# A gated recurrence followed by soft mixture-of-experts slots: a full, overlapping last group of tokens, a fourth decay buffer, another place for the copies of h, and another timetable for the weight loads

## The chip, the cores and the metric

The kernel runs on one core of one Trainium2 chip. A core has five engines that run side by side, each with its own in-order queue of instructions: TensorE (PE) multiplies and transposes, VectorE (DVE), ScalarE (ACT) and GpSimd (POOL) work elementwise, and SyncE (SP) issues transfers. Transfers run on 16 DMA engines. SBUF is the working memory of 128 partitions, PSUM the memory that TensorE writes to. The metric is the device time of one execution in microseconds; less is better. The times of the kernel before are 239.87, 241.03 and 241.69 us.

## The reference

Two stages. The first is a recurrence over 5056 tokens, for each of 4 batches and 256 channels; the second is a soft mixture of experts over all 20224 tokens, with 8 experts of 4 slots each.

```python
sig = 1.0 / (1.0 + np.exp(-f_logit))
f = lower_bound + (1.0 - lower_bound) * sig
i = 1.0 - f
for t in range(S):                       # y has the shape of x: (4, 5056, 256)
    h = f[:, t] * h + i[:, t] * x[:, t]
    y[:, t] = h

x = y.reshape(B * S, D)
logits = x @ phi                         # 20224 x 32
d = softmax of logits over the tokens (axis 0)
slot_input = (d.T @ x).reshape(E, S_per_e, D)
slot_out[e] = np.maximum(slot_input[e] @ w1[e], 0.0) @ w2[e]      # F = 1024
c = softmax of logits over the slots (axis 1)
out = c @ slot_out                       # 20224 x 256
```

All tokens must have gone through the recurrence and into the slots before the first output row can be made.

## The kernel before, in words

**Tiling.** The tokens of a batch are cut into groups of G = 1024, which is two halves (H = 2) of 512 (W), and a half is 128 partitions with R = 4 tokens each. 5056 tokens make four full groups and one of 960 tokens, which is held as two halves of 480 tokens on 120 partitions (`rows(4)` = 120). A unit is one group of one batch; there are 20 units, numbered `n = 4 * group + batch`.

**Phase one** (lines 115 to 332) is a software pipeline written out by hand: the loop at line 285 runs over steps n, and each step issues work of several units. For unit m:

- `load` (step m-5): one transfer of `f_t` and one of `x_t`, from SyncE's queue; three buffers each, so that `f_t` of unit m waits until the gate of unit m-3 is done, and `x_t` until its product is.
- `gate` (step m-2): ScalarE, sigmoid to `s_t`. `enter` (step m-2): GpSimd, product `u_t = s_t * x_t`.
- `s_to_channels` (end of step m-2) and `u_to_channels` (step m-1): eight TensorE transposes each, into PSUM tiles `sp` (one buffer, shared with the logits `lg`) and `up` (two buffers).
- `decay` (step m-1): two ScalarE instructions that write the decays `a` (three buffers), one for each half of the channels.
- `scan` (step m): two VectorE scans, one for each half of the channels, each starting from the last value of unit m-4 (same batch, group ahead). The last group, whose halves don't lie end to end, takes four scans.
- `to_tokens` and `keep_tokens` (step m+1): for each half of the tokens four TensorE transposes of `h` into `hp` (one buffer), and a copy to `ht`, by ScalarE for half 0 and by VectorE for half 1.

When a group's four units are scanned (`g1`), TensorE makes the logits and ScalarE the exponentials (`exps`, which needs another activation table, so the table is loaded before and after it). A step later (`g2`) the weights are transposed and copied (`et`), GpSimd sums them by row (`row_sums`), and the slots are accumulated (`slots`), with their second half a step later still (`g3`).

Every engine takes its work in the order in which the loop issues it. In the part of a step that the change touches, this order is: `load(n+5)`, `gate(n+2)`, `enter(n+2)`, weight loads, `u_to_channels(n+1)`, `decay(n+1)`, `weights_to_tokens(g2, 0)`, `scan(n, 0)`, `to_tokens(n-1, 0)`, `keep_tokens(n-1, 0)`, `keep_weights(g2, 0)`, and so on. So on ScalarE the copy of `h` of unit n-1 stands behind the decays of unit n+1.

**Weights.** The 16 weight loads (8 of `w1`, 8 of `w2`, each cast from float32 to bfloat16 on the way, 512 KB as written) are issued from GpSimd's queue at the steps of the table `W_AT`, behind that step's `enter`. Twelve of the sixteen are issued at step 17, behind the product of unit 19; the last four of `w2` go into load buffers that have come free.

**Tail and phase two.** The experts work on the slots (lines 335 to 408): the first layer needs all `w1`, and the second takes `w2` expert by expert (line 399). Then the output loop (line 415) multiplies the stored exponentials by the experts' result, scales by the row sums on VectorE or ScalarE, and stores each half unit from SyncE's queue: 128 partitions of 4 KB, in the last group 120.

Of the kernel before, what the change touches and what calls it, by code (L numbers as in the profile page):

```python
# [18 lines left out]
def kernel(  # L19
# [10 lines left out]
    nc = tc.nc  # L30
# [5 lines left out]
    P = 128  # L36
# [7 lines left out]
    n_unit = n_grp * B  # L44


    def rows(g):
        return min(P, (S - g * G) // (R * H))

    ctx.enter_context(tc.manual_schedule())  # L50

# [57 lines left out]
        nc.gpsimd.dma_start(out=w2_sb[e], in_=w2_r[e])  # L109


    W_AT = {8: 1, 13: 1, 15: 1, 16: 1, 17: 2 * E - 4}
    w_next = [0]

    with tc.tile_pool(name="sup", bufs=2) as sup, \
         tc.tile_pool(name="apool", bufs=3) as apool, \
         tc.tile_pool(name="hpool", bufs=6) as hpool, \
         tc.tile_pool(name="htok", bufs=7) as htok, \
         tc.tile_pool(name="etok", bufs=2) as etok, \
# [13 lines left out]

        def load(n):
            g, b = divmod(n, B)
            n_p = rows(g)
            fs[n] = ld.tile([P, H, R, D], F32, name="f_t", tag="f_t")
            xs[n] = ld.tile([P, H, R, D], F32, name="x_t", tag="x_t")
            for k in halves(n):
                for t, src in ((fs, f_logit), (xs, x)):  # L140
                    src = src[b, ds(g * G, n_p * R * H)]
                    src = src.rearrange("(h p r) d -> p h (r d)", h=H, r=R)
                    dst = t[n].rearrange("p h r d -> p h (r d)")
                    nc.sync.dma_start(out=dst[:n_p, k], in_=src[:, k])


        def gate(n):
            n_p = rows(n // B)
            sts[n] = sup.tile([P, H, R, D], BF16, name="s_t", tag="s_t")
            for k in halves(n):  # L150
                nc.scalar.activation(sts[n][:n_p, k], fs[n][:n_p, k], ACT.Sigmoid, scale=-1.0)  # L151

        def enter(n):
            n_p = rows(n // B)
            uts[n] = sup.tile([P, H, R, D], BF16, name="u_t", tag="u_t")
            eng = nc.vector if n == 0 else nc.gpsimd
            for k in halves(n):
                eng.tensor_tensor(uts[n][:n_p, k], sts[n][:n_p, k], xs[n][:n_p, k], ALU.mult)  # L158

        def to_channels(n, t, ps):  # L160
            n_p = rows(n // B)
            t = t.bitcast(F32)
            for h in range(H):
                for r in range(R):
                    nc.tensor.transpose(ps[:, h, :n_p, r], t[:n_p, h, r], ident_f[:n_p, :n_p])  # L165
            ps = ps.rearrange("c h p r -> c (h p r)").bitcast(BF16)
            return ps.rearrange("c (h t o) -> c h t o", h=H, o=DC)

        def s_to_channels(n):
            ps = ps_s.tile([P, H, P, R], F32, name="sp", tag="sp")  # L170
            sps[n] = to_channels(n, sts.pop(n), ps)

        def u_to_channels(n):
            ps = psu.tile([P, H, P, R], F32, name="up", tag="up")
            ups[n] = to_channels(n, uts.pop(n), ps)

        def flat(t, n_t):

            if n_t == W:
                return [t.rearrange("c h t -> c (h t)")]  # L180
            return [t[:, h, :n_t] for h in range(H)]

        def decay(n):
            n_t = rows(n // B) * R
            sp = sps.pop(n)
            for o in range(DC):
                a = apool.tile([P, H, W], F32, name="a", tag="a")
                nc.scalar.activation(a[:, :, :n_t], sp[:, :, :n_t, o], ACT.Identity,  # L188
                                     scale=nomlb[:, ds(o, 1)], bias=1.0)
                decays[n, o] = a  # L190

        def scan(n, o):
            n_t = rows(n // B) * R
            if o == 0:
                hs[n] = hpool.tile([P, H, W, DC], BF16, name="h", tag="h")
            carry = hs[n - B][:, H - 1, ds(W - 1, 1), o] if n >= B else 0.0
            for h, a, u in zip(flat(hs[n][:, :, :, o], n_t), flat(decays.pop((n, o)), n_t),
                               flat(ups[n][:, :, :, o], n_t)):
                nc.vector.tensor_tensor_scan(h, a, u, carry, ALU.mult, ALU.add)  # L199
                carry = h[:, ds(n_t - 1, 1)]  # L200

        def to_tokens(n, h):
            n_p = rows(n // B)
            hp = ptp.tile([P, R, P], F32, name="hp", tag="tp")
            hps[n, h] = hp
            hw = hs[n].bitcast(F32).rearrange("c h (p r) o -> c h p (r o)", r=R)
            for r in range(R):
                nc.tensor.transpose(hp[:n_p, r], hw[:, h, :n_p, r], ident_f)  # L208

        def keep_tokens(n, h):  # L210
            n_p = rows(n // B)
# [3 lines left out]
            copy(hts[n][:n_p, h].rearrange("p r d -> p (r d)").bitcast(F32),  # L215
                 hps.pop((n, h))[:n_p].rearrange("p r c -> p (r c)"))


        def logits(g):
            n_t = rows(g) * R  # L220
            lg = ps_s.tile([P, H, W], F32, name="lg", tag="sp")
            for h in range(H):
                for o in range(DC):
                    for b in range(B):
                        nc.tensor.matmul(lg[ds(b * NS, NS), h, :n_t], phi[:, o],  # L225
                                         hs[g * B + b][:, h, :n_t, o],
                                         start=o == 0, stop=o == DC - 1,
                                         skip_group_check=True)
            return lg

        def exps(g, lg):
            n_t = rows(g) * R
            nc.scalar.activation(etall[:, g, :, :n_t], lg[:, :, :n_t], ACT.Exp,
                                 accum_out=csum[:, ds(g, 1)])

        def weights(g, h):
            n_p = rows(g)
            return etall[:, g, h, :n_p * R].rearrange("s (p r) -> s p r", r=R)

        def weights_to_tokens(g, h):  # L240
            ew = weights(g, h)
            for r in range(R):
                nc.tensor.transpose(ep_ps[:rows(g), r], ew[:, :, r], ident)

        def keep_weights(g, h):
            n_p = rows(g)
            if h == 0:
                ets[g] = etok.tile([P, H, R, B, NS], BF16, name="et", tag="et")
            nc.vector.tensor_copy(ets[g][:n_p, h].rearrange("p r b s -> p (r b s)"),  # L249
                                  ep_ps[:n_p].rearrange("p r s -> p (r s)"))  # L250

        def row_sums(g):
            n_p, w = rows(g), NS // 2
            part = ets[g][:n_p].rearrange("p h r b s -> p (h r b) s")
            while w:
                if w == 1:
                    dst = rsum[:n_p, g].rearrange("p h r b -> p (h r b)").unsqueeze(2)
                else:
                    dst = rsp.tile([P, H * R * B, w], F32, name="rs", tag=f"rs{w}")[:n_p]
                nc.gpsimd.tensor_tensor(dst, part[:, :, :w], part[:, :, ds(w, w)], ALU.add)  # L260
                part, w = dst, w // 2

        def slots(g, h):
            n_p = rows(g)
# [20 lines left out]
        for n in range(-AHEAD, n_unit + 4):  # L285
            def has(m):
                return 0 <= m < n_unit
# [124 lines left out]
    with tc.tile_pool(name="pout", bufs=4, space=PSUM) as pout, \  # L412
         tc.tile_pool(name="osb", bufs=6) as osb:
        n_op = 0
        for n in range(n_unit):
            g, b = divmod(n, B)
            n_p = rows(g)
            dst = out[ds(b * S + g * G, n_p * R * H)]
            dst = dst.rearrange("(h p r) d -> p h r d", h=H, r=R)
            for h in range(H):  # L420
                op = pout.tile([P, R, D], F32, name="op", tag="op")
                ew = etall[:, g, h, :n_p * R].rearrange("s (p r) -> s p r", r=R)
                for r in range(R):
# [51 lines left out]
```

## Time and profile before

| | |
|---|---|
| median of three runs | 241.03 us |
| profiled execution | 241.04 us |
| its span, first to last instruction | 238.9 us |
| mean granted TensorE clock | 0.748 |
| busy: TensorE, VectorE, ScalarE, GpSimd | 144.7, 150.3, 135.5, 103.5 us |
| moved by DMA | 70.73 MB, mean 296 GB/s |
| scans of unit 0 begin, of unit 19 end | 11.65 us, 153.54 us |
| experts' result ready (`slot_out`) | 179.5 us |

Times in a profile are microseconds from the first instruction of the span. A line of the timeline has start and duration, engine, line of the kernel, operation, output and inputs, the number of merged instructions, and in brackets how long the engine was idle before it and what ended that idle time. "PEclk" or "granted clock" is the TensorE clock that the throttle granted, as a part of full speed. The DMA share is the mean busy share of the 16 DMA engines. A wait for several things is put down to the one that came last by the profile; where the engine named had long been done, it was another, often a transfer.

### The profile page before, as it was taken

To read this page: it belongs to the slowest core of one execution; us is meant where nothing else is said; L and a number is where in the kernel's file an instruction comes from. 1 tells how busy PE (TensorE), PEld (TensorE's weight loads), DVE (VectorE), ACT (ScalarE), POOL (GpSimd) and SP (SyncE) were. 2 spreads that over 40 slices of the span, in tenths; PEclk is the share of its full clock that TensorE was granted. 3 is DMA by queue.
4 is the path that set the end of the run, shared out by engine and by line. 5 is a ranking of instruction groups with operands and counts; after the bars stand their busy time and mean duration, and the time that the engine had idled before them with its cause. 6 is when DMAs were issued, how large, how long until landed. Compare 5 with 4: busy or idle time off the path is not lost.

```text
span 238.9 us, 2824 instructions
## 1 busy us (share of the span) xinstructions
PE 144.7 (61%) x1040; PEld 107.2 (45%) x1040; DVE 150.3 (63%) x128; ACT 135.5 (57%) x172; POOL 103.5 (43%) x68
## 2 busy tenths in 40 slices
PE   0637607663866568554868648378739877758600
PEld 0526607552754457543757537244515433325400
DVE  0465698886698966986888867722306654645520
ACT  3467807798578948799477934040106655254350
POOL 1057764627988289747995367166000000000000
PEclk9999975897699958998597968755875555555555
DMA  6999999995969986999999927999934999999995
GB/s 219 417 410 409 410 410 411 406 407 197 348 229 412 320 298 256 298 219 223 231 252 232 248 50 145 210 215 212 212 66 174 395 404 406 402 405 407 346 340 193
DMA packets 19357, 70.73 MB, mean 296 GB/s; under 512 B 1872, under 2 KB 1872, under 8 KB 19344
## 3 DMA queue, kind: packets, MB, share of 16 engines
q1 hardware_dynamic: 16752, 62.13, 72.0%
q0 software_dynamic: 2304, 8.39, 17.7%
q8 instruction: 8, 0.13, 0.2%
q10 hardware_dynamic: 288, 0.03, 0.1%
q14 instruction: 5, 0.04, 0.1%
HBM read 58.23 MB, written 20.71 MB: 330 GB/s over the span
## 4 chain that ended last, share of the span: by engine, by line
DMA 33%; ACT 22%; DVE 17%; PE 12%; issue 7%; SPq 3%; POOL 2%; ACTq 0%; DVEq 0%; POOLq 0%
DMA out_dram<-ob 12%; ACT a L188 9%; DMA x_t<-in_moe_w_dram 8%; DMA f_t<-in_f_logit_dram 8%; DVE h L199 8%; PE hp L208 5%; DMA w_sb_91<-in_moe_w_dram 5%; ACT ht L215 4%; PE sp L165 4%; ACT ob L432 3%; DVE ht L215 3%; DVE ob L435 3%; ACT s_t L151 3%; SPq L443 3%; DVE phi L79 2%
## 5 line engine op out<-in xcount | busy, mean ns | idle before, releaser
L158 POOL TENSOR_TENSOR u_t<-s_t,x_t 128x2048 bf16<-128x2048 bf16 (+1 forms) x19 | 78.1, 4108 | 50.8 <-ACT s_t L151 39.6
L199 DVE TENSOR_TENSOR_SCAN h<-a,h,up 128x1024 bf16<-128x1024 f32 (+1 forms) x40 | 74.3, 1884 | 0.3
L188 ACT ACTIVATE a<-sp,nomlb 128x1024 f32<-128x1024 bf16 (+1 forms) x40 | 42.8, 1099 | 32.9 <-PE sp L165 19.5
L208 PE MATMUL hp<-ident_f,h 128*128 128x128 f32 (+1 forms) x160 | 31.5, 327 | 33.0 <-ACT ht L215 29.2
L432 ACT ACTIVATE ob<-op,rrow 128x256 f32<-128x256 f32 (+1 forms) x68 | 26.4, 481 | 34.9 <-DVE ob L435 21.8
L151 ACT ACTIVATE s_t<-f_t 128x2048 bf16<-128x2048 f32 (+2 forms) x21 | 38.5, 1836 | 7.8 <-DMA f_t<-in_f_logit_dram 7.8
L424 PE MATMUL op<-slot_out,etall 32*128 32x256 bf16 (+1 forms) x160 | 36.4, 403 | 10.4 <-ACT ob L432 8.0
L435 DVE TENSOR_TENSOR ob<-op,rrow 128x1024 f32<-128x1024 f32 (+2 forms) x24 | 28.0, 1179 | 22.0 <-DMA out_dram<-ob 17.0
L208 PEld LDWEIGHTS hp<-ident_f,h 128*128 128x128 f32 (+1 forms) x160 | 24.2, 209 | 39.0 <-ACT ht L215 32.2
L165 PE MATMUL sp<-ident_f,s_t 128*128 128x128 f32 (+1 forms) x160 | 29.3, 342 | 15.1 <-ACT s_t L151 10.5
L424 PEld LDWEIGHTS <-etall 32*128 32x128 bf16 (+1 forms) x160 | 20.4, 146 | 26.8 <-issue 21.4
L165 PEld LDWEIGHTS sp<-ident_f,s_t 128*128 128x128 f32 (+1 forms) x160 | 23.7, 178 | 19.3 <-issue 8.3
L215 DVE COPY ht<-hp 128x512 f32<-128x512 f32 (+1 forms) x20 | 13.8, 690 | 26.5 <-PE hp L208 26.5
L165 PE MATMUL up<-ident_f,u_t 128*128 128x128 f32 (+1 forms) x160 | 27.0, 326 | 3.8 <-POOL u_t L158 3.8
L165 PEld LDWEIGHTS up<-ident_f,u_t 128*128 128x128 f32 (+1 forms) x160 | 23.8, 174 | 4.8 <-POOL u_t L158 4.8
L199 DVE TENSOR_TENSOR_SCAN h<-a,up 128x1024 bf16<-128x1024 f32 x8 | 17.8, 2273 | 5.9 <-PE up L165 5.9
L215 ACT COPY ht<-hp 128x512 f32<-128x512 f32 (+1 forms) x20 | 11.6, 582 | 8.0 <-PE hp L208 8.0
L267 PE MATMUL bank<-ht,et 128*32 128x256 bf16 (+1 forms) x160 | 8.6, 358 | 5.0 <-DVE et L249 5.0
L225 PE MATMUL lg<-h,phi 128*32 128x512 bf16 (+1 forms) x80 | 6.1, 431 | 7.0 <-ACT a L188 7.0
L267 PEld LDWEIGHTS <-et 128*32 128x32 bf16 (+1 forms) x160 | 5.0, 117 | 7.2 <-issue 6.1
L260 POOL TENSOR_TENSOR rs<-rs 128x256 f32<-128x256 f32 (+5 forms) x15 | 7.4, 491 | 1.2
L151 ACT ACT_TABLE_LOAD x5 | 6.4, 1283 | 1.7 <-PEq L459 1.7
(77 smaller groups left out, 92.4 us busy)
## 6 DMA issues: line engine op xcount, KB each, us to landing
f_t<-in_f_logit_dram SPq DMA_DIRECT2D x15, 1024.0 KB, 8.8
x_t<-in_x_dram SPq DMA_DIRECT2D x15, 1024.0 KB, 9.4
out_dram<-ob SPq DMA_DIRECT2D x30, 512.0 KB, 5.7
f_t<-in_f_logit_dram SPq DMA_DIRECT2D x4, 960.0 KB, 13.8
x_t<-in_x_dram SPq DMA_DIRECT2D x4, 960.0 KB, 14.6
out_dram<-ob SPq DMA_DIRECT2D x8, 480.0 KB, 6.6
f_t<-in_f_logit_dram SPq DMA_DIRECT2D x2, 512.0 KB, 5.0
x_t<-in_x_dram SPq DMA_DIRECT2D x2, 512.0 KB, 5.9
```

Of the source, the lines that this page charges most:

```text
L151: nc.scalar.activation(sts[n][:n_p, k], fs[n][:n_p, k], ACT.Sigmoid, scale=-1.0)
L158: eng.tensor_tensor(uts[n][:n_p, k], sts[n][:n_p, k], xs[n][:n_p, k], ALU.mult)
L165: nc.tensor.transpose(ps[:, h, :n_p, r], t[:n_p, h, r], ident_f[:n_p, :n_p])
L188: nc.scalar.activation(a[:, :, :n_t], sp[:, :, :n_t, o], ACT.Identity, scale=nomlb[:, ds(o, 1)], bias=1.0)
L199: nc.vector.tensor_tensor_scan(h, a, u, carry, ALU.mult, ALU.add)
L208: nc.tensor.transpose(hp[:n_p, r], hw[:, h, :n_p, r], ident_f)
L215: copy(hts[n][:n_p, h].rearrange("p r d -> p (r d)").bitcast(F32), hps.pop((n, h))[:n_p].rearrange("p r c -> p (r c)"))
L260: nc.gpsimd.tensor_tensor(dst, part[:, :, :w], part[:, :, ds(w, w)], ALU.add)
L267: nc.tensor.matmul(slot_ps[ds(b * NS, NS), :], ets[g][:n_p, h, r, b], hts[g * B + b][:n_p, h, r], start=(h == 0 and r == 0), stop=(h == H ...
L424: nc.tensor.matmul(op[:n_p, r], ew[ds(b * NS, NS), :, r], slot_out[ds(b * NS, NS), :], start=True, stop=True, skip_group_check=True)
L432: nc.scalar.activation(ob[:n_p, r], op[:n_p, r], ACT.Copy, scale=rrow[:n_p, g, h, r, ds(b, 1)])
L435: nc.vector.tensor_tensor(ob[:n_p, r], op[:n_p, r], rrow[:n_p, g, h, r, ds(b, 1)].broadcast_to([n_p, r.stop - r.start, D]), ALU.mult)
```

## The change

Four things are changed.

1. The last group has 1024 tokens like the others. It starts at S - G = 4032 (`first`), 64 tokens ahead of where the fourth group ends. All units load, gate and scan 1024 tokens. The fourth group, units 12 to 15, scans its 1024 tokens but uses the first 960 (`used`) in the second stage: half 0 has 128 rows, half 1 has 112. The carry of the last group is taken at token 960 of the fourth. The row sums of the fourth group are made in two parts, since its halves differ in rows.
2. The pool of the decays has four buffers instead of three.
3. `to_tokens(n-1, 0)` and `keep_tokens(n-1, 0)` stand ahead of the weight loads, `u_to_channels(n+1)`, `decay(n+1)` and `scan(n, 0)` of their step. On TensorE the four transposes come ahead of those of `u`, and on ScalarE the copy comes behind the gate and ahead of the decays.
4. Weight loads are issued at steps 2, 5, 8, 11, 13, 15 and 16, one each, and nine at step 17, instead of one each at 8, 13, 15 and 16 and twelve at 17.

```diff
+    def first(g):
+        return g * G if g < n_grp - 1 else S - G
+    def used(g):
+        return first(g + 1) - first(g) if g < n_grp - 1 else G
-    def rows(g):
-        return min(P, (S - g * G) // (R * H))
+    def rows(g, h):
+        return min(P, (used(g) - h * W) // R)
...
-    W_AT = {8: 1, 13: 1, 15: 1, 16: 1, 17: 2 * E - 4}
+    W_AT = {2: 1, 5: 1, 8: 1, 11: 1, 13: 1, 15: 1, 16: 1, 17: 2 * E - 7}
...
-         tc.tile_pool(name="apool", bufs=3) as apool, \
+         tc.tile_pool(name="apool", bufs=4) as apool, \
...
-                    src = src[b, ds(g * G, n_p * R * H)]
+                    src = src[b, ds(first(g), G)]
...
-                    nc.sync.dma_start(out=dst[:n_p, k], in_=src[:, k])
+                    nc.sync.dma_start(out=dst[:, k], in_=src[:, k])
...
-            carry = hs[n - B][:, H - 1, ds(W - 1, 1), o] if n >= B else 0.0
-            for h, a, u in zip(flat(hs[n][:, :, :, o], n_t), flat(decays.pop((n, o)), n_t),
-                               flat(ups[n][:, :, :, o], n_t)):
-                nc.vector.tensor_tensor_scan(h, a, u, carry, ALU.mult, ALU.add)
-                carry = h[:, ds(n_t - 1, 1)]
+            carry = 0.0
+            if n >= B:
+                h, t = divmod(used(n // B - 1) - 1, W)
+                carry = hs[n - B][:, h, ds(t, 1), o]
+            nc.vector.tensor_tensor_scan(
+                hs[n].rearrange("c h t o -> c (h t) o")[:, :, o],
+                decays.pop((n, o)).rearrange("c h t -> c (h t)"), ups[n][:, :, o],
+                carry, ALU.mult, ALU.add)
...
+            same = rows(g, 0) == rows(g, H - 1)
+            for k in [ds(0, H)] if same else [ds(h, 1) for h in range(H)]:
+                n_p, w = rows(g, k.start), NS // 2
...
             if has(n + 2):
                 gate(n + 2)
                 enter(n + 2)
+            if has(n - 1):
+                to_tokens(n - 1, 0)
+                keep_tokens(n - 1, 0)
             for _ in range(W_AT.get(n, 0)):
                 load_w(w_next[0])
...
             if has(n):
                 scan(n, 0)
-            if has(n - 1):
-                to_tokens(n - 1, 0)
-                keep_tokens(n - 1, 0)
...
-            dst = out[ds(b * S + g * G, n_p * R * H)]
+            dst = out[ds(b * S + first(g), G)]
...
-                    nc.sync.dma_start(out=dst[:, h, k], in_=ob[:n_p, k])
+                    nc.sync.dma_start(out=dst[:n_p, h, k], in_=ob[:n_p, k])
```

More of the change, by code (lines that the diff above doesn't have):

```diff
@@ L157, in enter, with to_channels @@
             for k in halves(n):
[L158 to L161 removed]
+                eng.tensor_tensor(uts[n][:, k], sts[n][:, k], xs[n][:, k], ALU.mult)
+        def to_channels(t, ps):
             t = t.bitcast(F32)
@@ L164, in to_channels @@
                 for r in range(R):
-                    nc.tensor.transpose(ps[:, h, :n_p, r], t[:n_p, h, r], ident_f[:n_p, :n_p])
+                    nc.tensor.transpose(ps[:, h, :, r], t[:, h, r], ident_f)
             ps = ps.rearrange("c h p r -> c (h p r)").bitcast(BF16)
@@ L170, in s_to_channels @@
             ps = ps_s.tile([P, H, P, R], F32, name="sp", tag="sp")
-            sps[n] = to_channels(n, sts.pop(n), ps)
+            sps[n] = to_channels(sts.pop(n), ps)
         def u_to_channels(n):
             ps = psu.tile([P, H, P, R], F32, name="up", tag="up")
[L175 to L181, printed above, removed]
+            ups[n] = to_channels(uts.pop(n), ps)
         def decay(n):
-            n_t = rows(n // B) * R
             sp = sps.pop(n)
@@ L210, in keep_tokens @@
         def keep_tokens(n, h):
-            n_p = rows(n // B)
+            n_p = rows(n // B, h)
             if h == 0:
@@ L219, in logits @@
         def logits(g):
-            n_t = rows(g) * R
             lg = ps_s.tile([P, H, W], F32, name="lg", tag="sp")
             for h in range(H):
+                n_t = rows(g, h) * R
                 for o in range(DC):
@@ L231, in exps @@
         def exps(g, lg):
[L232 to L238, printed above, removed]
+            nc.scalar.activation(
+                etall[:, g].rearrange("s h t -> s (h t)")[:, :used(g)],
+                lg.rearrange("s h t -> s (h t)")[:, :used(g)], ACT.Exp,
+                accum_out=csum[:, ds(g, 1)])
         def weights_to_tokens(g, h):
-            ew = weights(g, h)
+            n_p = rows(g, h)
+            ew = etall[:, g, h, :n_p * R].rearrange("s (p r) -> s p r", r=R)
             for r in range(R):
-                nc.tensor.transpose(ep_ps[:rows(g), r], ew[:, :, r], ident)
+                nc.tensor.transpose(ep_ps[:n_p, r], ew[:, :, r], ident)
         def keep_weights(g, h):
-            n_p = rows(g)
+            n_p = rows(g, h)
             if h == 0:
```

33 lines of the change are left out of this document (15 added, 18 removed).

## The prediction

> **What bounds the kernel now.** I read the page's slices first, then the timeline of each engine over one whole group, then the last weights. A unit is 1024 tokens of one batch, a group is four units. The page:
>
> ```profile
> span 238.9 us, 2824 instructions
> ...
> DMA  6999999995969986999999927999934999999995
> ...
> q0 software_dynamic: 2304, 8.39, 17.7%
> ```
>
> DMA is nearly always busy, yet not always with useful speed. The next four lines are the DMA view over 100 to 113 us (only 120-row loads of the last group in flight), the same view over 40 to 53 us (only 128-row loads), and two stretches of the output phase, 128-row and then 120-row stores (columns of the windows: engines' busy time with counts, granted TensorE clock, DMA share, GB/s):
>
> ```profile
> DMA packets 748, 2.89 MB, mean 222 GB/s; under 512 B 45, under 2 KB 45, under 8 KB 747
> DMA packets 1371, 5.30 MB, mean 408 GB/s; under 512 B 79, under 2 KB 79, under 8 KB 1370
> 186.00:216.00 30.00, 22.04 (x95) 10.88 (x93) 16.32 (x14) 13.94 (x36) 0.00 (x0) 0.50 1.02 405
> 224.00:236.00 12.00, 1.82 (x8) 1.28 (x7) 3.12 (x3) 3.14 (x8) 0.00 (x0) 0.50 0.93 325
> ```
>
> So a last-group unit of 1.97 MB takes 1.966/0.222 = 8.86 us, a full one of 2.10 MB takes 2.097/0.408 = 5.14 us. In the middle of phase one, however, DMA has gaps and VectorE sets the pace. Its timeline (start, us, engine, line, operation, in brackets the idle time before it):
>
> ```profile
> 33.53 4.45 DVE L199 TENSOR_TENSOR_SCAN h<-a,up 128x1024 bf16<-128x1024 f32 x2
> ...
> 44.95 4.58 DVE L199 TENSOR_TENSOR_SCAN h<-a,h,up 128x1024 bf16<-128x1024 f32 x2
> ...
> 72.23 4.58 DVE L199 TENSOR_TENSOR_SCAN h<-a,h,up 128x1024 bf16<-128x1024 f32 x2
> 77.58 0.69 DVE L215 COPY ht<-hp 128x512 f32<-128x512 f32 x1 [0.77 <-PE hp L208]
> ...
> 80.90 0.42 DVE L249 COPY et<-bank 128x512 bf16<-128x512 bf16 x1 [0.37 <-PE bank L243]
> ...
> 85.55 0.69 DVE L215 COPY ht<-hp 128x512 f32<-128x512 f32 x1 [1.97 <-PE hp L208]
> ...
> 93.16 0.69 DVE L215 COPY ht<-hp 128x512 f32<-128x512 f32 x1 [2.10 <-PE hp L208]
> ...
> 98.91 0.69 DVE L215 COPY ht<-hp 128x512 f32<-128x512 f32 x1 [0.23 <-PE hp L208]
> 99.52 4.58 DVE L199 TENSOR_TENSOR_SCAN h<-a,h,up 128x1024 bf16<-128x1024 f32 x2
> ...
> 127.14 4.81 DVE L199 TENSOR_TENSOR_SCAN h<-a,h,up 128x480 bf16<-128x480 f32 x4
> ...
> 148.72 4.82 DVE L199 TENSOR_TENSOR_SCAN h<-a,h,up 128x480 bf16<-128x480 f32 x4
> ```
>
> The scan pairs shown are those of units 2, 4, 8, 12, 16 and 19. From unit 8 to unit 12 is 99.52 - 72.23 = 27.29 us, and the waits in it are 0.77 + 0.37 + 1.97 + 2.10 + 0.23 = 5.44; VectorE's own work is 21.85 per group. A plain unit is 4.58 + (99.52 - 98.91) = 5.19. What those waits wait for is on ScalarE and TensorE:
>
> ```profile
> 74.60 1.11 ACT L188 ACTIVATE a<-sp,nomlb 128x1024 f32<-128x1024 bf16 x1 [0.99 <-DVE h L199]
> 75.61 0.58 ACT L215 COPY ht<-hp 128x512 f32<-128x512 f32 x1
> 76.21 1.28 ACT L233 ACT_TABLE_LOAD   x1
> 77.50 1.02 ACT L233 ACTIVATE etall<-lg 128x1024 bf16<-128x1024 f32 x1
> ...
> 78.64 1.28 ACT L151 ACT_TABLE_LOAD   x1
> 79.93 1.91 ACT L151 ACTIVATE s_t<-f_t 128x2048 bf16<-128x2048 f32 x1
> 81.75 2.11 ACT L188 ACTIVATE a<-sp,nomlb 128x1024 f32<-128x1024 bf16 x2
> 83.74 0.59 ACT L215 COPY ht<-hp 128x512 f32<-128x512 f32 x1
> ```
>
> ```profile
> 75.77 1.09 PE L225 MATMUL lg<-h,phi 128*32 128x512 bf16 x16 [1.96 <-ACT a L188]
> ...
> 78.67 1.09 PE L165 MATMUL sp<-ident_f,s_t 128*128 128x128 f32 x8 [1.13 <-ACT etall L233]
> ...
> 84.38 1.13 PE L208 MATMUL hp<-ident_f,h 128*128 128x128 f32 x4 [2.62 <-ACT ht L215]
> ...
> 87.60 1.97 PE L165 MATMUL sp<-ident_f,s_t 128*128 128x128 f32 x8
> ...
> 98.12 0.75 PE L208 MATMUL hp<-ident_f,h 128*128 128x128 f32 x4 [2.06 <-ACT ht L215]
> ```
>
> With three buffers `a`, every second decay waits for a scan (0.99 in the first line), and the copy of `h` stands behind both decays on ScalarE. The one PSUM buffer `hp` is free only after that copy, so the second half's transposes, VectorE's copy of them and the next scans follow late. After the exponentials it is worst: table load, gate, two decays, and only at 83.74 the copy. TensorE idles 2.62 us there and comes back at half clock:
>
> ```profile
> 90.00:108.00 18.00, 12.15 (x115) 10.49 (x114) 14.72 (x10) 15.71 (x16) 12.15 (x3) 0.97 0.87 255
> 108.00:112.00 4.00, 1.40 (x13) 1.08 (x11) 2.68 (x2) 4.00 (x5) 2.78 (x1) 0.94 0.96 223
> 112.00:118.00 6.00, 4.89 (x35) 4.11 (x34) 5.16 (x4) 2.53 (x3) 5.59 (x8) 0.50 1.00 225
> ```
>
> The end of phase one and the tail (GpSimd's last product and first of the twelve late weight loads; first, fifth and last expert sets on TensorE; VectorE's copy that follows):
>
> ```profile
> 139.26 4.09 POOL L158 TENSOR_TENSOR u_t<-s_t,x_t 120x2048 bf16<-120x2048 bf16 x1 [5.61 <-ACT ht L215]
> 143.31 0.59 POOL L101 DMA_DIRECT2D w_sb_88<-in_moe_w_dram  x1
> 170.09 0.40 PE L399 MATMUL so_ps<-w_sb_92,hid 128*32 128x256 bf16 x8
> ...
> 170.97 0.39 PE L399 MATMUL so_ps<-f_t,hid 128*32 128x256 bf16 x8
> ...
> 176.60 0.62 PE L399 MATMUL so_ps<-x_t,hid 128*32 128x256 bf16 x8 [2.14 <-DMA x_t<-in_moe_w_dram]
> 177.27 0.42 DVE L405 COPY so_1605<-so_ps 128x256 f32<-128x256 f32 x1 [5.70 <-PE so_ps L399]
> ```
>
> Unit 19's product waits for its slow 120-row load (the page names a ScalarE copy that was long over), the weights are queued behind that product, and the last weight ends the tail.
>
> **Phase one up to unit 4.** Units 2 to 4 are bare of group work. Between 33.53 and 44.95 two units pass in 11.42 us; with the copy of `h` no longer late they take 2 x 5.19, so unit 4 starts at 43.91.
>
> **The h copies and the fourth buffer, per group.** Set zero at the end of the scan ahead of a step with logits. VectorE's copy 0.61, four transposes 0.75, ScalarE's copy 0.58 and two decays 2.11, now without a buffer wait, give 4.05. Logits 1.09 and the other half's transposes 0.75 end at 5.89; the scan pair ends at 0.61 + 4.58 = 5.19. VectorE waits 0.70 (0.77 before). ScalarE's exponential table goes beside the logits to 5.33, exponential to 6.47 (78.64 - 77.50 = 1.14), table 7.75, gate 9.66, and now the copy, 10.24, ahead of the decays; the transposes end at 10.99. VectorE starts its scan at 6.50 and halfway waits for the weights' transposes: 0.37 before, at most 0.75 more since `hp` now stands ahead of them; I take 0.70. Its next copy is due at about 12.2, so the wait of 1.97 goes. That copy and the second `et` end at 13.2.
>
> What is late next is the wait of 2.10. From 13.2 TensorE does slots (as short as the logits, 1.09), `sp`, `hp`, the transposes of `u` (as `sp`) and `hp`; the scan pair ends at 17.8. At full clock that is 1.09 + 1.09 + 0.75 + 1.09 + 0.75, to 18.0: a wait of 0.2. At half clock it is 1.09 + 1.97 + 1.13 + 1.97 + 1.13, to 20.5: 2.7. Which clock? TensorE's gap is now 13.2 - 10.99 = 2.2 us; 2.06 left the clock up (98.12), 2.62 came with it down, and in both gaps the few matmuls before matter too (1.40 us busy in 108 to 112). The stretch before mine is as thin as that one, so I take the half clock, with part of the time recovered as it was by 90 us: 1.5. The Trainium skill, "TensorE: Matmul & The Clock Gate", section "Why this matters for your kernels", asks for no idle gap over about 3 us; the trace drops the clock after 2.62, so it is stricter here, and by the page alone the sum would be the full-clock rival's.
>
> Group: 21.85 + 0.70 + 0.70 + 1.5 = 24.75 (full clock 23.45), against 27.29. The remaining wait of 0.23 goes: at full or half clock ScalarE's copy precedes its decays there.
>
> What covers the rest: the decays now begin after the copy, at 1.94, and are needed 3 us later. The transposes of `u` stand behind `hp` on TensorE and need only be there a unit later. GpSimd has 4 x 4.1 of products (row 139.26) plus row sums in 24.75; a weight's issue adds 0.59 to it.
>
> **Full last group.** Unit 16 starts at 43.91 + 3 x 24.75 = 118.16, and unit 19's scans end at 118.16 + 24.75 - 5.19 + 4.58 = 142.30 (before: 148.72 + 4.82 = 153.54). This holds if loads are not late. They need 20 x 5.14 and the five weights at steps 2 to 13, each 17.7% x 238.9/16 = 2.64: 116 us of transfers. Unit 19's gate begins at 118.16 - 0.61 + 7.75 = 125.3 and ends at 127.2, so there are some 9 us of room; before, the 120-row loads took 4 x (8.86 - 5.14) = 14.9 more, and had none. The 64 tokens more per batch cost nothing on the engines (their time goes by columns; the full scan pair, 4.58, is shorter than four short scans, 4.81). Row sums of the cut group come in two parts on an idle GpSimd.
>
> **Weights.** Unit 19's product ends at 127.2 + 4.09 = 131.3. Twelve weights took 176.60 - 143.31 = 33.29 from there; nine take 33.29 - 3 x 2.64 = 25.4, to 156.7. Without its weight wait, the eighth expert set would have ended at 170.09 + 7 x 0.22 + 0.40 = 172.03, the copy at 172.08, which is 18.54 after unit 19's scans. After: 142.30 + 18.54 = 160.84. The weights are there 4 us earlier; the tail is then bound by compute.
>
> **Outputs.** From that copy to the end is 238.9 - 177.27 = 61.63. The eight 480 KB stores took 3.93/0.325 = 12.1 instead of 9.7 at 405 GB/s. Full rows save that 2.4. No trace has 112-row stores (four, 1.84 MB): at 325 they give back 1.1, at the loads' 222 they give back 3.7. Between +1.3 and -2.4, I take -1.0, near the store row.
>
> **Sum.** 160.84 + 61.63 - 1.0 = 221.5 of span; the profiled execution took 241.04 for 238.9, so 2.14 on top: **223.6 us**. The median, 241.03, is the same as that execution.
>
> **Rivals.**
> Full clock throughout: groups of 23.45 put unit 16 at 114.26, the copy at 114.26 + 22.84 + 18.54 = 155.64, the weights at 152.8, and the time at 218.4. For it: the gap is nearer to 2.06 than to 2.62. Against: the thin work around it.
>
> The weights at steps 2 and 5 fall where DMA is at 9 tenths in every slice, and mixed traffic may be slower than its parts: if the three weights moved ahead of the last load delay every scan after them, that is 3 x 2.64 more, 231.5. Against: units are loaded three ahead, and VectorE, not DMA, lags from 33 us on.
>
> The group stays at 27.29, because another order of waits (GpSimd's products, one `sp` buffer) replaces the old: 43.91 + 4 x 27.29 - 0.61 + 18.54 gives the copy at 171.0, and 233.8 in all.
>
> Slower: the new order closes a ring. The copy now stands ahead of the decays, these free the one `sp` buffer, its transposes stand ahead of the next `hp`, and that feeds the next copy. At half clock a step of it takes 1.13 + 0.58 + 2.11 + 1.97 = 5.79, over VectorE's 5.19. With logits and both slots doubled (3 x 2.18) and the exponential 1.14, a group is about 31, the copy comes at 186, and the time is 249. It decides from a group of 29.1 on, which gives 241. Against it: 90 to 108 us, mostly transposes, ran at 0.97. The Trainium skill, same page, section "Part 4: PE-mode transpose", says that transposes do not engage the full clock, which would mean this ring; that row contradicts it.
>
> **Chances.** Forecast 0.48, full clock 0.27, late loads 0.12, group unchanged 0.08, ring 0.05. All but the last are faster by over 1%, about what a measurement of this kernel can tell; I leave 0.02 for a mixture near zero. The range goes from full clock with the best stores and a little less waiting, 215.5, to just beyond the late loads, 232; outside are the last two cases.
>
> **What would show it.** Unit 8 to unit 12 in about 24.7 us on VectorE, without a 1.97 wait; no decay waiting for a scan; TensorE's clock at 0.5 after each group's step or not; the last group's loads at about 400 GB/s; unit 19's product near 127 to 131 and not waiting for DMA; the last expert set not waiting for a weight; stores at 400 GB/s to the end. It would be wrong if VectorE's scans show waits for products or loads in steps that carry a weight, or if TensorE's clock stays low between groups.

## The result, and the profile after

The changed kernel takes 217.95 us (median of four runs, 217.30 to 218.55), the kernel before beside it 240.45 us. The ratio is 0.9063, with a 95% interval from 0.9006 to 0.9120. The forecast was 223.6 us, in a range from 215.5 to 232. In five of the variants below some runs took over 1.5% longer than the fastest of the same kernel, and the ratios leave these runs out.

By stage, in the profiled executions:

| point in the span, us | before | forecast | after |
|---|---|---|---|
| scans of unit 4 begin | 44.95 | 43.91 | 43.50 |
| of unit 8 | 72.23 | 68.66 | 67.34 |
| of unit 12 | 99.52 | 93.41 | 90.67 |
| of unit 16 | 127.14 | 118.16 | 114.36 |
| scans of unit 19 end | 153.54 | 142.30 | 137.69 |
| copy behind the last expert set | 177.27 | 160.84 | 156.48 |
| end of span | 238.9 | 221.5 | 216.0 |

The page of the kernel after:

```profile
span 216.0 us, 2801 instructions
...
PEclk9999997696999988999699979755795555555555
DMA  6999999999999999999999849999129999999996
```

DMA now runs without a gap to the end of the loads. VectorE's timeline over the same group as before, from unit 8 to unit 12, and the scans of units 16 and 19:

```profile
67.34 4.58 DVE L197 TENSOR_TENSOR_SCAN h<-a,h,up 128x1024 bf16<-128x1024 f32 x2
72.75 0.69 DVE L215 COPY ht<-hp 128x512 f32<-128x512 f32 x1 [0.83 <-PE hp L208]
...
76.07 0.42 DVE L247 COPY et<-bank 128x512 bf16<-128x512 bf16 x1 [0.37 <-PE bank L241]
...
84.66 0.69 DVE L215 COPY ht<-hp 128x512 f32<-128x512 f32 x1 [0.50 <-PE hp L208]
...
90.67 4.58 DVE L197 TENSOR_TENSOR_SCAN h<-a,h,up 128x1024 bf16<-128x1024 f32 x2
...
114.36 4.58 DVE L197 TENSOR_TENSOR_SCAN h<-a,h,up 128x1024 bf16<-128x1024 f32 x2
...
133.11 4.58 DVE L197 TENSOR_TENSOR_SCAN h<-a,h,up 128x1024 bf16<-128x1024 f32 x2
```

The group takes 90.67 - 67.34 = 23.33 us, with 1.70 us of waits where there were 5.44. The wait of 1.97 is gone altogether, that of 2.10 is 0.50. TensorE and ScalarE in the same group:

```profile
79.71 1.04 PE L268 MATMUL bank<-ht,et 128*32 128x256 bf16 x16 [1.91 <-DVE et L247]
80.69 1.97 PE L169 MATMUL sp<-ident_f,s_t 128*128 128x128 f32 x8
82.45 0.74 PE L208 MATMUL hp<-ident_f,h 128*128 128x128 f32 x4
83.03 1.04 PE L169 MATMUL up<-ident_f,u_t 128*128 128x128 f32 x8
```

```profile
74.61 1.91 ACT L157 ACTIVATE s_t<-f_t 128x2048 bf16<-128x2048 f32 x1
76.44 0.57 ACT L215 COPY ht<-hp 128x512 f32<-128x512 f32 x1
76.90 2.12 ACT L185 ACTIVATE a<-sp,nomlb 128x1024 f32<-128x1024 bf16 x2
```

ScalarE's copy of `h` now stands between the gate and the decays. TensorE does come back at half clock after its gap of 1.91 us (slots 1.04, `sp` 1.97), but the very next transposes run at full clock again (0.74, and 1.04 for `u`). The end of phase one and the tail (GpSimd's product of unit 19 and the first weight behind it; the last two expert sets, which share one line; the copy):

```profile
123.85 4.10 POOL L163 TENSOR_TENSOR u_t<-s_t,x_t 128x2048 bf16<-128x2048 bf16 x1 [2.44 <-ACT s_t L157]
127.91 0.59 POOL L109 DMA_DIRECT2D w_sb_91<-in_moe_w_dram  x1
155.82 0.61 PE L400 MATMUL so_ps<-x_t,hid 128*32 128x256 bf16 x16
156.48 0.43 DVE L406 COPY so_1606<-so_ps 128x256 f32<-128x256 f32 x1 [0.50 <-PE so_ps L400]
```

Unit 19's product waits for ScalarE's gate, no longer for a load, and no expert set waits for a weight.

### The profile page after: what moved, and what is told of

Its sections match the earlier page's. It is cut to its first block, busy times and chain, and to the rows that moved or that the text cites. A ratio compares the mean times of both kernels' runs of the same rounds, so it can differ in the third digit from the quotient of the medians.

```text
span 216.0 us, 2801 instructions
## 1 busy us (share of the span) xinstructions
PE 137.6 (64%) x1040; PEld 101.3 (47%) x1040; DVE 149.7 (69%) x120; ACT 134.3 (62%) x172; POOL 104.4 (48%) x73
## 4 chain that ended last, share of the span: by engine, by line
DVE 24%; ACT 24%; PE 23%; DMA 17%; issue 5%; SPq 3%; DVEq 0%; ACTq 0%
DVE h L197 10%; DMA out_dram<-ob 10%; ACT a L185 9%; PE sp L169 6%; DMA f_t<-in_f_logit_dram 5%; DVE ob L436 5%; PE hp L208 5%; ACT s_t L157 4%; ACT ob L433 3%; SPq L444 3%; PE up L169 3%; ACT L232 3%; DVE ht L215 3%; ACT etall L232 3%; PE bank L268 2%
## 5 line engine op out<-in xcount | busy, mean ns | idle before, releaser
L163 POOL TENSOR_TENSOR u_t<-s_t,x_t 128x2048 bf16<-128x2048 bf16 x19 | 78.1, 4117 | 35.1 <-ACT s_t L157 32.0
L197 DVE TENSOR_TENSOR_SCAN h<-a,h,up 128x1024 bf16<-128x1024 f32 x32 | 73.7, 2335 | 0.0
L157 ACT ACTIVATE s_t<-f_t 128x2048 bf16<-128x2048 f32 (+1 forms) x21 | 38.6, 1836 | 8.6 <-DMA f_t<-in_f_logit_dram 8.6
L185 ACT ACTIVATE a<-sp,nomlb 128x1024 f32<-128x1024 bf16 x40 | 42.6, 1122 | 1.7 <-DVE nomlb L78 1.7
L169 PE MATMUL sp<-ident_f,s_t 128*128 128x128 f32 x160 | 28.2, 331 | 18.4 <-ACT s_t L157 10.5
L169 PEld LDWEIGHTS sp<-ident_f,s_t 128*128 128x128 f32 x160 | 22.0, 169 | 23.7 <-ACT a L185 7.5
L169 PE MATMUL up<-ident_f,u_t 128*128 128x128 f32 x160 | 24.4, 303 | 7.5 <-POOL u_t L163 7.5
L215 ACT COPY ht<-hp 128x512 f32<-128x512 f32 x20 | 11.7, 584 | 23.8 <-PE hp L208 23.8
L169 PEld LDWEIGHTS up<-ident_f,u_t 128*128 128x128 f32 x160 | 20.8, 158 | 9.6 <-POOL u_t L163 9.6
L197 DVE TENSOR_TENSOR_SCAN h<-a,up 128x1024 bf16<-128x1024 f32 x8 | 17.8, 2271 | 5.9 <-PE up L169 5.9
L261 POOL TENSOR_TENSOR rs<-rs 128x128 f32<-128x128 f32 (+6 forms) x18 | 7.9, 440 | 1.4
```

What stands on the lines that cost most here:

```text
L157: nc.scalar.activation(sts[n][:, k], fs[n][:, k], ACT.Sigmoid, scale=-1.0)
L163: eng.tensor_tensor(uts[n][:, k], sts[n][:, k], xs[n][:, k], ALU.mult)
L169: nc.tensor.transpose(ps[:, h, :, r], t[:, h, r], ident_f)
L185: nc.scalar.activation(a, sp[:, :, :, o], ACT.Identity, scale=nomlb[:, ds(o, 1)], bias=1.0)
L197: nc.vector.tensor_tensor_scan(hs[n].rearrange("c h t o -> c (h t) o")[:, :, o], decays.pop((n, o)).rearrange("c h t -> c (h t)"), ups[n][ ...
```

## The experiments

**One part left out at a time.** All four kernels are the changed kernel with one part undone.

Without the full last group. This is the kernel before with the parts 2, 3 and 4 of the change. Its last group has 960 tokens again, as two halves of 480 on 120 partitions, in loads, scans, row sums and stores.

> The change without its full last group: 120-row loads, four short scans, 120-row stores, the other three parts kept. Theory: the loads of units 16 to 19 need 4 x 8.86 us from about 93 us on, with three weights of 2.64 beside them, so unit 19's product begins near 136 us instead of 123.85; its scans, the tail and the slower stores give about 230 to 233 us, and GpSimd waits for unit 19's load. Rival, the last group's loads are hidden by the three load buffers: only the stores get slower, 220 us.

Measured: 229.23 us (227.32 to 230.72), ratio to the kernel before 0.9448 (0.9382 to 0.9514). The DMA view from 95 to 140 us, then ScalarE's table load ahead of unit 19's gate and GpSimd's product of unit 19:

```profile
GB/s 193 218 226 222 215 233 255 273 226 222 200 237 211 229 200 237 266 251 288 200 218 215 218 204 211 215 211 237 211 218 226 269 233 280 255 229 204 164 69 7
```

```profile
133.05 1.28 ACT L151 ACT_TABLE_LOAD   x1 [3.19 <-DMA f_t<-in_f_logit_dram]
138.08 4.09 POOL L158 TENSOR_TENSOR u_t<-s_t,x_t 120x2048 bf16<-120x2048 bf16 x1 [6.27 <-PE hp L208]
```

Loads crawl at 200 to 280 GB/s for 43 us, and the last product begins at 138.08, 14 us after that of the changed kernel and only 1.2 before that of the kernel before (the transposes that the line names had long been done; the gate ahead of it had waited 3.19 us for `f_t`). The three load buffers do not hide it. The first theory holds, with a time 0.8 us below its range: without this part, the faster groups end in front of a load.

Without the fourth decay buffer:

```diff
-         tc.tile_pool(name="apool", bufs=4) as apool, \
+         tc.tile_pool(name="apool", bufs=3) as apool, \
```

> The change with three decay buffers instead of four, all else kept. Theory: the copy of h now stands ahead of the decays, so the second decay begins about 3.05 us after the scans of the unit ahead, and the buffer it needs is free after 2.9 us; under 0.5 us per group, 218 to 220 us. Rival, the fourth buffer is the main part: a wait of about 1 us in each of 16 steps, up to 230 us or more.

Measured: 216.86 us (215.81 to 217.09), ratio 0.8955 (0.8918 to 0.8991), which is not slower than the change, and is below the 218 to 220 us of the first theory; by the ratios it is 1% faster, by the medians 0.5%. The decays' group in the view by lines, and the one decay that waited for a scan:

```profile
L185 ACT ACTIVATE a<-sp,nomlb 128x1024 f32<-128x1024 bf16 x40 | 42.7, 1122 | 7.3 <-DVE h L197 5.6 <-DVE nomlb L78 1.7
35.83 1.11 ACT L185 ACTIVATE a<-sp,nomlb 128x1024 f32<-128x1024 bf16 x1 [5.61 <-DVE h L197]
```

All of the 5.6 us is one wait, at 35.83, before the pipeline is full; with four buffers it is not there. From then on no decay waits for a scan, since the copy now stands ahead of the decays, and that one wait costs nothing: the scans of unit 8 begin at 66.92, in the change at 67.34. Why the kernel came out faster is not settled. From the end of unit 19's scans to the instruction that writes `slot_out` its tail takes 17.8 us, the change's 20.0. The windows of the two tails (this kernel first; the last three columns are granted clock, DMA share and GB/s):

```profile
137.00:155.00 18.00, 12.56 (x184) 7.91 (x185) 6.35 (x16) 4.45 (x7) 5.16 (x9) 0.91 0.87 175
```

```profile
137.70:158.00 20.30, 16.56 (x184) 10.18 (x185) 6.42 (x15) 4.44 (x7) 5.06 (x8) 0.59 0.76 153
```

The same work met a TensorE clock of 0.91 here and 0.59 there; what shifted the clock was not tested.

With the copies of `h` where they were:

```diff
             if has(n):
                 scan(n, 0)
+            if has(n - 1):
+                to_tokens(n - 1, 0)
+                keep_tokens(n - 1, 0)
```

> The change with the copies of h where they were, behind the decays and, on TensorE, behind the transposes of u; four decay buffers kept. Theory: VectorE's waits for the second half's transposes come back after each group's exponentials (about 1.1 and 2.0 us), groups of about 26 us instead of 23.6, 225 to 229 us. Rival, the fourth buffer by itself ends the delay: 218 to 220 us.

Measured: 221.85 us, and 225.67 to 226.90 us in the three runs left out; one run gives no ratio. VectorE's copies in the group from unit 8 to 12, which took 25.3 us (the profile is of the run of 226.90 us):

```profile
L215 DVE COPY ht<-hp 128x512 f32<-128x512 f32 x5 | 3.4, 674 | 3.8 <-PE hp L208 3.8
```

The 3.8 us of waits at the copies (1.84 and 1.98), against 1.3 in the change, are the ones that the theory brings back, and the kernel before, with its copies in the same place, shows the same two (1.97 and 2.10). The fourth buffer alone does not end them. By the run of 221.85 us the move is worth 4 us, not the 7 to 11 that were expected; why the other three runs are longer stays open.

With the old timetable of the weights:

```diff
-    W_AT = {2: 1, 5: 1, 8: 1, 11: 1, 13: 1, 15: 1, 16: 1, 17: 2 * E - 7}
+    W_AT = {8: 1, 13: 1, 15: 1, 16: 1, 17: 2 * E - 4}
```

> The change with the old timetable of the weight loads, twelve at step 17. Theory: unit 19's product ends near 127.5 us as with the change, the twelve weights end 33.3 us later, near 161, and the copy behind the last expert set comes there instead of at 156.5: 222 to 223 us, with the last expert set waiting for a weight. Rival, the weights put early hold up loads and products in phase one: without them unit 19's scans end some microseconds before 137.7, and the total is 219 or less.

Measured: ratio 0.9310 (0.9250 to 0.9369); the two runs in it took 224.46 and 226.01 us, 1.5 us and more above the 222 to 223 expected. The lines are of a run of 228.83 us.

```profile
125.81 4.10 POOL L163 TENSOR_TENSOR u_t<-s_t,x_t 128x2048 bf16<-128x2048 bf16 x1 [3.45 <-ACT s_t L157]
129.86 2.19 POOL L109 DMA_DIRECT2D w_sb<-in_moe_w_dram  x4
```

```profile
158.09 0.40 PE L400 MATMUL so_ps<-f_t,hid 128*32 128x256 bf16 x8 [1.84 <-DMA f_t<-in_moe_w_dram]
160.53 0.62 PE L400 MATMUL so_ps<-x_t,hid 128*32 128x256 bf16 x8 [2.04 <-DMA x_t<-in_moe_w_dram]
163.03 0.62 PE L400 MATMUL so_ps<-x_t,hid 128*32 128x256 bf16 x8 [1.89 <-DMA x_t<-in_moe_w_dram]
```

The last expert sets wait for weights one after another, and the last comes 33.2 us after the first late issue, as reckoned. The rival falls: the time is far over its 219, and without early weights phase one is no faster. In the profiled run the last product even begins 2 us later than in the change, and what delays it stays open.

**One part alone.** All three are the kernel before with one part of the change.

```
full_only:    the full last group;  three decay buffers, copies and weights as before
buf_move:     bufs=4 and the moved copies;  last group and weights as before
spread_only:  the new W_AT;  all else as before
```

> The kernel before with the full last group alone. Theory: groups stay at about 27.3 us, unit 19's load comes in time, which takes away the waits of 2.8 and 2.4 us for it, the twelve weights still end 33 us after unit 19's product, and the stores gain 2: 235 to 238 us. Rival, the parts simply add up (what the change loses without this part, 11 us, is what this part gains alone): 230 us.

> The kernel before with the fourth decay buffer and the moved copies alone. Theory: groups of 23.6 us, but units 16 to 19 wait for their 120-row loads, unit 19's product ends near 142 us as with these loads in the change, and twelve weights follow it, 33 us: 175 us where it was 176.6, so 238 to 241 us, next to nothing gained. Rival, the parts add up: 8 us gained, 233 us.

> The kernel before with the new timetable of the weights alone. Theory: the weights end 8 us earlier after unit 19's product, of which the last expert set can use about 5 before compute binds; three more weights ahead of the slow 120-row loads give some of it back: 236 to 240 us. Rival, the parts add up: 9 us gained, 232 us.

| alone | us (all runs) | ratio (95%) | last product begins | copy behind the experts |
|---|---|---|---|---|
| full last group | 234.91 to 238.65 | 0.9777 (0.9695 to 0.9859) | 135.69 | 173.03 |
| buffer and move | 234.07 to 237.79 | 0.9728 (0.9660 to 0.9796) | 132.81 | 170.58 |
| weights | 236.38 to 238.77 | 0.9811 (0.9754 to 0.9869) | 141.37 | 176.64 |
| all (the change) | 217.30 to 218.55 | 0.9063 (0.9006 to 0.9120) | 123.85 | 156.48 |

2.2%, 2.7% and 1.9% sum to 6.8%; together they give 9.4%. The difference is about twice what the intervals leave open, so the parts do not simply add up, they enable each other, as the first theories say; the full group and the weights alone fall into the ranges given. Buffer and move alone, from which next to nothing was expected, gained 2.7% (236.2 us instead of 238 to 241): with only two weights ahead of the last loads instead of five, unit 19's product begins 5 us earlier than without the full group in the change, from which this kernel differs in the timetable alone. In that kernel the last two expert sets wait for weights on TensorE:

```profile
167.42 0.40 PE L399 MATMUL so_ps<-x_t,hid 128*32 128x256 bf16 x8 [2.06 <-DMA x_t<-in_moe_w_dram]
169.91 0.62 PE L399 MATMUL so_ps<-x_t,hid 128*32 128x256 bf16 x8 [2.09 <-DMA x_t<-in_moe_w_dram]
```

With the weights alone it is the other way round: no expert set waits, but the last product is 2.1 us later than before, with three weights more ahead of the slow loads. So the rival of late loads in the prediction is real, but only beside 120-row loads.

**Why the 120-row loads are slow.** First each is cut in two:

```diff
-                    nc.sync.dma_start(out=dst[:n_p, k], in_=src[:, k])
+                    if n_p == P:
+                        nc.sync.dma_start(out=dst[:n_p, k], in_=src[:, k])
+                    else:
+                        nc.sync.dma_start(out=dst[:112, k], in_=src[:112, k])
+                        nc.sync.dma_start(out=dst[112:n_p, k], in_=src[112:, k])
```

> The kernel before with each 120-row load issued as one of 112 rows and one of 8. If the slow rate is due to 120 rows as such (sixteen engines cannot share them evenly), the big part runs at about 400 GB/s, f_t and x_t land in 6 to 9 us instead of 13.8 and 14.6, and the time falls by 2 to 4 us. If it is due to the last group's place and strides in memory (halves of 480 tokens), DMA stays near 222 GB/s in the stretch in which only these loads are in flight, and the time stays.

Measured in one run: 240.02 us, where the kernel before took 240.69 to 242.96 beside it. The big parts land in 11.3 and 13.2 us, and DMA moves 239 GB/s from 100 to 110 us. That fits the second explanation, the place in memory, but also a slowness of any number of rows below 128. So the next run keeps 120 rows and changes the place:

```diff
-                    src = src[b, ds(g * G, n_p * R * H)]
+                    src = src[b, ds(min(g * G, S - G), G)]
-                    nc.sync.dma_start(out=dst[:n_p, k], in_=src[:, k])
+                    nc.sync.dma_start(out=dst[:n_p, k], in_=src[:n_p, k])
```

> The kernel before, where the last group's loads take 120 rows per half at the places of a full group that starts at token 4032 (halves 512 tokens apart; the last eight rows of each half are left out, so the last group works on other tokens). If the slow rate is due to the number of rows, the stretch with only these loads in flight stays near 222 GB/s; if it is due to halves 480 tokens apart or to the place, it runs at about 400 GB/s and f_t lands in 9 us instead of 13.8.

Measured in one run: 243.44 us. The DMA view from 100 to 113 us, and after it SyncE's queue in the kernel before from 40 to 53 us, with 128-row loads only:

```profile
DMA packets 702, 2.72 MB, mean 209 GB/s; under 512 B 42, under 2 KB 42, under 8 KB 701
...
q1 hardware_dynamic: 701, 2.70, 95.6%
```

```profile
q1 hardware_dynamic: 1370, 5.29, 101.9%
```

At the very places at which the change loads, 120 rows move 209 GB/s. It is the rows: full 128-row transfers run at about 410, and with 120 rows the 16 engines are nearly as busy (95.6% against 101.9%) and move half. The stores agree: while the four stores of 112 rows pass among full ones, DMA is full and moves 359 GB/s instead of 404 (windows of the kernel after):

```profile
175.00:188.00 13.00, 9.93 (x41) 5.18 (x40) 6.90 (x6) 6.27 (x16) 0.00 (x0) 0.50 1.02 404
188.00:204.00 16.00, 10.83 (x46) 5.86 (x45) 8.84 (x8) 6.26 (x16) 0.00 (x0) 0.50 1.00 359
```

The Trainium skill, "DMA: Bandwidth & Descriptors", section "Why a DMA increments its semaphore by 16 and not by 1", gives a transfer the largest number of engines up to 16 that divides its rows, which is 15 for 120 rows and 16 for 112 or 128. The trace agrees: 95.6% is 15/16 of 101.9%, and the 16752 packets of SyncE's queue in the kernel before come out with 15 packets beyond the data for each 120-row transfer and 16 for each other one. But a missing engine would cost a sixteenth, and the runs show a half. What makes each engine slower stays open.

**What is late next.** TensorE's gap is filled with transposes made three times over:

```diff
-            for r in range(R):
+            for r in list(range(R)) * times:
                 nc.tensor.transpose(hp[:n_p, r], hw[:, h, :n_p, r], ident_f)
...
-                to_tokens(n - 1, 1)
+                to_tokens(n - 1, 1, 1 if g2 is None else 3)
```

> The change, and in the step after the logits the four transposes of the second half of h are made three times over, with the same result, so that TensorE works through most of its 2 us gap. Theory: the gap is why its clock falls to half; filled, the slots and the transposes of s behind them run at full clock (0.62 and 1.09 us instead of 1.04 and 1.97) and VectorE's wait of 0.5 to 0.7 us a little later goes: 215 to 217 us. If that wait were worth 1.5 us as predicted, 212 to 213 us. Rival, the clock does not follow this gap: still 1.97 us and 218 us or a little more.

Measured: 217.07 us (216.42 to 217.44), ratio 0.8977 (0.8933 to 0.9021). TensorE one group later than shown above:

```profile
99.69 1.57 PE L208 MATMUL hp<-ident_f,h 128*112 128x128 f32 x12
102.40 0.62 PE L268 MATMUL bank<-ht,et 128*32 128x256 bf16 x16 [1.14 <-DVE et L247]
102.95 1.09 PE L169 MATMUL sp<-ident_f,s_t 128*128 128x128 f32 x8
...
111.26 1.56 PE L169 MATMUL up<-ident_f,u_t 128*128 128x128 f32 x8 [2.46 <-POOL u_t L163]
```

With the gap at 1.14 us the clock stays up (0.62 and 1.09), here and in the other three groups, and VectorE's wait behind it is gone. So the half clock needs the gap. But the gap is not enough: in the change itself, in the group from unit 4, it was 2.25 us long behind the same transposes, and the clock stayed up:

```profile
57.00 0.62 PE L268 MATMUL bank<-ht,et 128*32 128x256 bf16 x16 [2.25 <-DVE et L247]
57.55 1.09 PE L169 MATMUL sp<-ident_f,s_t 128*128 128x128 f32 x8
```

Seven of the profiled kernels have the moved copies and this gap unfilled, 1.90 to 2.25 us long, in 26 groups together. In 18 of them some of the work behind the gap ran at half clock, in eight none did. What else decides was not tested.

Filling the gap is worth little: the group from unit 8 takes 22.89 us instead of 23.33, but in the next one TensorE waits 2.46 us for a product of GpSimd, whose products and row sums run end to end there, and ScalarE 1.57 for a load; that group takes 24.35.

```profile
113.04 1.91 ACT L157 ACTIVATE s_t<-f_t 128x2048 bf16<-128x2048 f32 x1 [1.57 <-DMA f_t<-in_f_logit_dram]
```

In that group GpSimd and DMA both come into the way of a faster VectorE.

Then the other wait of VectorE:

```diff
-            if g1 is not None:
+            if g1 is not None and not has(n):
                 exps(g1, logits(g1))
...
                 to_tokens(n - 1, 1)
                 keep_tokens(n - 1, 1)
+            if g1 is not None and has(n):
+                exps(g1, logits(g1))
```

> The change, and in a step with logits the transposes of the second half of h stand ahead of the logits on TensorE, not behind. Theory: VectorE's wait there (0.91, 0.83, 1.04, 0.98 us) goes, the logits still wait for the decays and are not later: about 1 us per group, 213 to 216 us, groups of 22.7 us. Rival, GpSimd's products set the pace (its products and row sums run end to end for about 19 of 23.6 us): another wait takes the place, 217 to 218 us as with the change.

> The same with three decay buffers instead of four. Theory: no decay waits longer than 0.1 us for a scan once the copies stand ahead of the decays; the same time within 1%. Rival, a step with faster scans needs the fourth buffer: 2 us slower.

Measured: ratio 0.9043 (0.8974 to 0.9111) with four decay buffers and 0.9047 (0.8995 to 0.9099) with three, the same as the change within its interval, and the same with either number of buffers. VectorE's view by lines of the first, from unit 8 to unit 12:

```profile
L215 DVE COPY ht<-hp 128x512 f32<-128x512 f32 x5 | 3.4, 671 | 1.0 <-PE hp L208 1.0
L247 DVE COPY et<-bank 128x512 bf16<-128x512 bf16 x2 | 0.8, 418 | 1.3 <-PE bank L241 1.3
```

The wait of 0.83 at the copy is gone, and that at `et` has grown from 0.4 to 1.3: the exponentials begin at 72.22 as in the change (72.19), since they hang on ScalarE's chain of copy, decays and table load. VectorE merely arrives sooner and waits there. The 1.0 that is left at a copy is of a later step, and there the rival shows. TensorE waits 1.88 us for a product of GpSimd, whose products and row sums run end to end from 76.65 to 92 us, and comes back at half clock:

```profile
88.02 1.71 PE L169 MATMUL up<-ident_f,u_t 128*128 128x128 f32 x8 [1.88 <-POOL u_t L163]
```

So the theory falls, and the rival holds in part: one wait took the place behind ScalarE and one behind GpSimd. Of all that was run, the changed kernel with three buffers has the lowest median, 216.86 us, and that with the filled gap (217.07) is the same within the intervals.

## Why the prediction was right or wrong

The sum missed by 223.6 - 217.94 = 5.66 us: 4.61 up to the end of unit 19's scans, 1.11 in the output phase and 0.20 around the span, less 0.25 in the tail.

- **Up to unit 4** (43.91): 43.50. Right.
- **Waits that stay**: 0.70 at the logits was 0.83 to 1.04, and 0.70 at `et` was 0.37 to 0.50 from unit 8 on. The 1.97 went, as said. Together right from unit 8 on; in the group from unit 4 the wait at `et` was 1.43, behind transposes at half clock.
- **The wait of 2.10, forecast at 1.5, was the step that failed, by its size.** It was 0.50, 0.58 and 0.72 in the three groups from unit 8 on, and nothing in the group from unit 4. The half clock came in those three, as forecast, but not in the first, with a longer gap (2.25 us) behind the same thin work. So the argument from the thin work was right in part by luck; in the profile before the clock was down, too, behind a gap of 2.11 us with more work ahead of it (at 125.36). The full-clock rival's 218.4 is nearest to the result, though its clock was met in one group of four: where the half clock came, it covered only the slots and `sp` (the two lines of 1.04 and 1.97) and little of the operations behind them. The recovery was taken from the profile before, where TensorE was slow from 84.38 to about 91; after, it was back 2.7 us after the stage began. With 0.6 in place of 1.5 and the measured 0.9 and 0.45 a group is 23.8 instead of 24.75; measured were 23.84 from unit 4 on, then 23.33 and 23.69.
- **Full last group**: right, and the part without which the change loses most (alone it gains 2.2%, buffer and move 2.7%). Its loads run at full speed, unit 19's product begins at 123.85 (forecast 127.2) and waits for no load. Without it 3.9% of the time before are lost. That the last group's load is what phase one ends on was in the trace before, in the 222 GB/s.
- **Weights**: right. They were forecast to be there 4 us ahead of the last expert set, and no set waits. By the variant without this part, it is worth 2.5%.
- **The h copies and the fourth buffer** were costed together; the runs part them. The move carries what there is, and beside it the buffer carries nothing. The buffer without the rest was not tried.
- **Outputs**: -1.0 forecast, -2.1 measured (59.52 from the copy to the end of the span, against 61.63). Of the 2.1, 0.9 lies ahead of the first output: it comes 2.44 us after that copy instead of 3.37, with TensorE no longer at half clock there (0.70 us instead of 1.22 for the two matmuls behind the copy). The stores themselves gain about 1.2, near the forecast, so the 112-row stores cost less than the full last rows gain.
- **Rivals**: late loads did not come (the last product waits for the gate), nor did the ring at half clock. The sentence of the Trainium skill, "TensorE: Matmul & The Clock Gate", section "Part 4: PE-mode transpose", that transposes do not engage the full clock does not hold here: filling the gap with transposes kept it up (0.62 and 1.09 us behind it in all four groups).
- **GpSimd** was called idle enough. It is, for the change, but with 1.1 to 1.3 us of TensorE's waits for its products per group it is next in line, and in the run with the filled gap it is what TensorE waits for longest (2.46 us).

## What to carry to other kernels

When a stretch shows DMA full but at half its usual rate, look at the shape of its transfers first: a last tile that overlaps its neighbour and keeps all 128 rows was worth 3.9% beside the other parts and 2.2% alone, at the price of computing 64 tokens twice. Changes that each remove one of several waits in series can be worth less alone than together, so read from the trace which wait is next before judging a part by itself. On an in-order engine, put the short instruction that frees a single buffer ahead of the long ones that don't; more buffers for the long ones then buy nothing.

## What the runs showed of the hardware

Loads of 120 rows of 2 x 4 KB move 209 to 222 GB/s where 128 rows move about 408, with the DMA engines nearly as busy, and also at the addresses of the full group (one run); cutting off 8 rows doesn't cure it (239 GB/s). TensorE's granted clock can fall to half after a gap of 1.9 us: behind gaps of 1.90 to 2.25 us and the same work it did in 18 groups of 26 and didn't in eight. Where transposes filled the gap down to 1.11 to 1.14 us, it stayed up in four groups of four.
